# Filter sums in the first transform stage, tap and cross sums by accumulating transfers, a fused gate, and a second norm turned by transfers

## The chip, the cores and the metric

One Trainium2 chip, one core. The metric is device time of one execution in microseconds (us). TensorE is called PE here, VectorE DVE, ScalarE ACT, GpSimd POOL, SyncE SP, as the profile calls them. POOL and SP also issue transfers: POOL's are the profile's queue q0 (software), SP's the queue q1 (hardware).

## The reference, cut to what matters

A layer norm, a convolution block with a gate, a residual, a second layer norm and a SwiGLU feed-forward block, on a sequence of S = 2048 rows of D = 640 columns.

```python
x = A_q                                          # [1, 2048, 640]
k_shift[s] = sum over t of k[s - 3 + t] * shift_k[:, 3 - t]      # four taps
kv = k_shift * v
y  = causal convolution of kv with ssm_k along S, + kv * ssm_D    # by FFT in the reference
h  = x + layernorm(x) * y
out = h + (silu(layernorm(h) @ w_gate) * (layernorm(h) @ w_up)) @ w_down    # F = 1728
```

## The kernel before, in words

The sequence is cut into four blocks of 512 rows (j = 0 to 3), the columns of the convolution into two halves of 320 (c = 0, 1). A tile holds 512 rows as 128 partitions x 4 rows. The causal convolution works on spectra of 1024 points: block j of the output needs the products of the spectra X(i) of kv and K(m) of the filter with i + m = j, and K(m) must stand for filter blocks m and m-1 together.

For each block and half the kernel goes through these steps.

- **Taps** (`kv_block`, line 909): four products of 1280 columns and three sums, all on DVE through the helper at line 756, and one product with v. One block-half is eight DVE instructions.
- **Filter** (`load_kraw`, line 614): the filter block is turned by a transposing transfer (line 620) and laid out again by way of DRAM (`k_nat`).
- **First transform stage** (`fwd`, line 670): 8 matmuls of 320 columns per tile, evacuations on ACT, then four shuffles within SBUF by transfers on SP's queue. **Second stage** (`spec`, line 741): 4 matmuls for each of four groups of frequencies (h = 0 to 3).
- **Filter sum** (`shift_add`, line 747): two DVE instructions of 640 columns add the spectra of filter blocks j and j-1.
- **Products** (`products`, line 758; `combine`, line 792): complex products of 1280 columns, added up on DVE over the pairs (i, m). Block 2 also computes two pairs ahead for block 3. Then `inv2` and `conv_bp` transform back.
- **Gate and residual** (`conv_bp`, line 1006): ACT (or DVE) makes layernorm(x) (line 877), DVE multiplies it with y from PSUM (640 columns) and adds the residual (640 columns).
- **Second norm** (`ln_bp`, line 1051): the normalised rows are turned by 10 PE transposes (line 1063) and copied out of PSUM by ACT or DVE into HNT.
- **Feed-forward** (`ffn_pair`, `ffn_b`, lines 1090 and 1126): for a block, 135 matmuls of 512 columns and 112 of 320, with SiLU on ACT (line 1103) and a product of 1024 columns on DVE.

Block 0 has a dense transform instead (`dense_c`, line 708). Its tables lie in the space of spectra that are not used yet. PSUM is cut into two pools of two slots, pF for the feed-forward and pC for the convolution.

The order of all instructions is written out at build time by a list planner in the kernel (`Prog.schedule`, line 131). It gives each operation a cost, a priority (1000 j + 100 c + ... for the convolution, 10000 + 100 j for the feed-forward) and, for transfers, a modelled landing. Each engine and each queue then runs its list strictly in order, waiting at an instruction until what it depends on is done. On POOL that list holds the loads of k, v, x and of all weights, each weight piece waiting for the piece two before it, and the power instruction of the layer norms (line 867). So whatever waits on POOL holds all loads behind it.

```python
def piece(subs, kb, cells, nm):
    chain.append(dma(subs, kb, [], cells, 35, eng="pool", after=chain[-2:-1] or [kv_last[0, 0]], name=nm))
```

Of the kernel before, what the change touches and what calls it, by code (L numbers as in the profile page):

```python
# [40 lines left out]
class Prog:  # L41
# [196 lines left out]
    def emit(self, nc, es, block, ndma_sems):  # L238
# [4 lines left out]
        for e in self.ENG:  # L243
            n = 0
# [23 lines left out]
        for e in self.ENG:  # L268
            prog, seen, owed = [], {}, 0
            for o in self.order[e]:  # L270
# [15 lines left out]
                for tl in {x[0] for x in o.writes}:  # L286
                    for p in tl.prev:
                        wrote = any(x[0] is not None and x[0].base == tl.base and x[0].pool == tl.pool for x in p.writes)
                        need(p, 2 if wrote else 1)
# [54 lines left out]
def _tables(R):  # L344
# [4 lines left out]
    for T in range(2):  # L349
        f1 = (64 * T + np.arange(64))[None, :] + 0.5  # L350
        s1f[:, T, 0:64] = np.cos(2 * np.pi * q * f1 / 256)
        s1f[:, T, 64:128] = -np.sin(2 * np.pi * q * f1 / 256)
    s1i = np.stack([s1f[:, T, :].T for T in range(2)], axis=1)
# [18 lines left out]
    cols = [s1f.reshape(128, -1), s1i.reshape(128, -1), w2s, w2i.reshape(128, -1), np.eye(128)]  # L372
# [31 lines left out]
def bass_sequential_preLN__ssm_conv_h3__swiglu_ffn__prompt_kernel(  # L404
# [18 lines left out]
    tab_np, (oS1, oS1I, oW2, oW2I, oID) = _tables(R)  # L423
# [8 lines left out]
    with ExitStack() as es:  # L432
        NEL = 102720
        sb = es.enter_context(nc.sbuf_tensor("sb", [128, NEL], bf))
        tab = es.enter_context(nc.sbuf_tensor("tab", [128, tab_np.shape[1]], f16))
        stt = es.enter_context(nc.sbuf_tensor("stt", [128, 192 + 32 + 192 + 8], f32))
        ps = es.enter_context(nc.psum_tensor("ps", [128, 4096], f32))
        psb = ps[:].bitcast(bf)
        cur = [0]
# [10 lines left out]
        def V(t, off, n, p0=0, p1=128):  # L450
            return sb[p0:p1, t.base + off:t.base + off + n]

# [44 lines left out]
        P.pool("TMP", slots(2, 4 * CW), True)  # L497
        P.pool("KRAW", slots(1, 3 * B), True)
        P.pool("KT", slots(2, 4 * CW), True)
        P.pool("TK", slots(2, 8 * CW), True)  # L500
        P.pool("TX", slots(3, 8 * CW), True)
        sx, sxb = slots(2, 8 * CW), slots(2, 8 * CW)
        skb, sk = slots(2, 8 * CW), slots(2, 8 * CW)
        P.pool("SX", sx + sxb, True)
        P.pool("SK", sk + skb, True)
        DEN = P.tile("den", None, sxb[0])
# [7 lines left out]
        P.pool("SS", slots(5, 4 * CW), True)  # L514
        P.pool("PP", slots(3, 4 * CW), True)
        P.pool("P0", [HNT.base + i * 2 * CW for i in range(4)], True)
        P.pool("EP", slots(3, 2 * CW), True)
        P.pool("JK", slots(1, 2 * CW), True)
        P.pool("pF", [0, 1024])
        P.pool("pC", [2048, 3072])  # L520
# [55 lines left out]
        for k in range(4):  # L576
            def tap(k):
                pt = P.tile("ptap", "pC" if k % 2 else "pF")
# [35 lines left out]
        def load_kraw(j, c, prio):  # L614
# [11 lines left out]
            if (j, c) == (0, 1):  # L626
                t = kraws[j, c] = P.tile("kraw01", None, GUT.base + 11 * CW)
            else:
                t = kraws[j, c] = P.tile(f"kraw{j}{c}", "KRAW")
# [10 lines left out]
        def k_natural(j, c, prio):  # L640
# [6 lines left out]
            pt = P.tile("pKT", "pC")  # L647
# [22 lines left out]
        def fwd(nm, srcs, pool, prio):  # L670

            tbt = P.tile("TB" + nm, pool)
            for b in range(4):
                pt = P.tile("p1", "pC")
# [23 lines left out]
        def dense_h(nm, src, h, dst, prio):  # L698
            pt = P.tile("pd", "pC")
# [8 lines left out]
        def dense_c(c):  # L708
# [7 lines left out]
            acc = [P.tile(f"y{c}{i}", "pF") for i in range(2)]  # L716
            for h in range(R):
                dense_h(f"X{c}", vins[0, c], h, xt, pb + 103)
                a1, a2 = products([(xt, h * 640, kt, h * 640)], [h], "P0", pb + 110, f"0{c}{h}")
                combine((a1, a2), lambda a1=a1: V2(a1, 0, 640, 1, CW), lambda a2=a2: V2(a2, 0, 640, 1, CW), 1, [(a1, 0)], [(a2, 0)],  # L720
                        pb + 110, f"0{c}{h}")
                fns = []
                for ri, a in enumerate((a1, a2)):
                    for b in range(R):
                        fns.append(mm(lambda b=b: B32(acc[b // 2], b % 2, CW), lambda h=h, ri=ri, b=b: den(oIV(h, ri, b)),
                                      lambda a=a: V(a, 0, CW), h == 0 and ri == 0, h == R - 1 and ri == 1))
                last = pe(fns, CW, 8, [(a1, 0), (a2, 0), (DEN, ("i", h))], [(acc[0], 0), (acc[1], 0)], pb + 110, name=f"di{c}h{h}")
# [13 lines left out]
        def spec(nm, r, u, h, dst, off, prio):  # L741
            pt = P.tile("p2", "pC")
            pe(stage2(u, h, pt), CW, 2, [(u, h), (TAB, 1)], [(pt, 0)], prio, reserve=[(dst, h)], name=f"s2{r}{nm}h{h}", mode=1)
            evac(lambda: V2(dst, off, CW, 2, CW), lambda: B32x2(pt, CW), 2 * CW, [(pt, 0)], [(dst, h)], prio,
                 name=f"e2{r}{nm}h{h}", after=[den_last[0]])

        def shift_add(dst, do, cur_, co, prv, po, hs, prio, nm):
            rd = [(t, h) for t in (cur_, prv) for h in hs]
            wr = [(dst, h) for h in hs]
            o1 = vec(dve2(640), tt(lambda: V2(dst, do, 960, 2, CW), lambda: V2(cur_, co, 960, 2, CW), lambda: V2(prv, po + CW, CW, 2, CW), ALU.subtract),  # L750
                     rd, [(dst, (h, "a")) for h in hs], prio, name=f"ks{nm}")
            vec(dve2(640), tt(lambda: V2(dst, do + CW, CW, 2, CW), lambda: V2(cur_, co + CW, CW, 2, CW), lambda: V2(prv, po, 960, 2, CW), ALU.add),
                rd + [(dst, (h, "a")) for h in hs], wr, prio, name=f"kp{nm}")
# [4 lines left out]
        def products(terms, hs, pool, prio, nm):  # L758


            n = len(hs)
            accs = None
            for n_, (xt, xo, kt, ko) in enumerate(terms):
                p1 = P.tile(f"P1{nm}", pool)
                p2 = P.tile(f"P2{nm}", pool) if n_ == 0 else None
                rd = [(xt, h) for h in hs] + [(kt, h) for h in hs]

                def m1(dst, xt=xt, xo=xo, kt=kt, ko=ko, rd=rd):
                    vec(dve2(640 * n), tt(lambda: V(dst, 0, 640 * n), lambda: V(xt, xo, 640 * n), lambda: V(kt, ko, 640 * n), ALU.mult),
                        rd, [(dst, i) for i in range(n)], prio, name=f"m1{nm}")  # L770

                def m2(dst, xt=xt, xo=xo, kt=kt, ko=ko, rd=rd):
                    vec(dve2(640 * n), tt(lambda: V3(dst, 0, 640, n, CW, 2, CW), lambda: V3(xt, xo, 640, n, CW, 2, CW),
                                          lambda: V3(kt, ko + CW, 640, n, -CW, 2, CW), ALU.mult),
                        rd, [(dst, i) for i in range(n)], prio, name=f"m2{nm}")

                def add(a, b_):
                    vec(dve2(640 * n), tt(lambda: V(a, 0, 640 * n), lambda: V(a, 0, 640 * n), lambda: V(b_, 0, 640 * n), ALU.add),
                        [(t, i) for t in (a, b_) for i in range(n)], [(a, i) for i in range(n)], prio, name=f"ac{nm}")

                m1(p1)
                if n_ == 0:
                    m2(p2)
                    accs = (p1, p2)
                else:
                    add(accs[0], p1)
                    q2 = P.tile(f"P2{nm}", pool)
                    m2(q2)
                    add(accs[1], q2)
            return accs  # L790

        def combine(accs, dre, dim, n, wre, wim, prio, nm, after=()):
            a, b_ = accs
            ra, rb = [(a, i) for i in range(n)], [(b_, i) for i in range(n)]
            o1 = vec(dve2(CW * n), tt(dre, lambda: V2(a, 0, 640, n, CW), lambda: V2(a, CW, 640, n, CW), ALU.subtract),
                     ra, wre, prio, name=f"cr{nm}")
            vec(dve2(CW * n), tt(dim, lambda: V2(b_, 0, 640, n, CW), lambda: V2(b_, CW, 640, n, CW), ALU.add),
                rb, wim, prio, name=f"ci{nm}", after=[o1])
# [440 lines left out]
```

## Time and profile before

| what | value |
|---|---|
| times of three runs | 325.8, 326.7 (median), 331.81 us |
| span of the profiled execution, first to last instruction | 329.1 us |
| busy: PE, DVE, ACT, POOL | 284.9, 251.0, 184.7, 40.8 us |
| 1280-column DVE instructions on SBUF | 176, 140.3 us busy |
| 640-column DVE instructions on SBUF | 96, 44.7 us busy |
| first instruction of the feed-forward of block 0 / 1 / 2 / 3 | 64.9 / 137.9 / 225.2 / 281 us |
| end of the last matmul | 325.9 us |

The profiled execution's own total is not listed beside its span; its span is 2.4 us above the median of the times. The columns of the table of windows are: stretch, its length, busy time and (x instructions) of PE, PEld (weight load), DVE, ACT and POOL, the granted PE clock as a share of full speed, the busy share of the transfer engines, and GB/s. In a timeline a line is: start, length, engine, line, operation, output<-input, count, and in brackets the idle time before it and what ended that. "128x1280" is partitions x elements. Since two instructions of an engine overlap a little, the distance from start to start (the pitch) is smaller than the duration of one.

### The profile page before, as it was taken

How to read it: one execution, taken by the hardware profiler on the slowest of the kernel's cores; microseconds unless marked ns; L12 is line 12 of the kernel's file. 1: busy time of each engine (PE TensorE's matmuls, PEld its weight loads, DVE VectorE, ACT ScalarE, POOL GpSimd, SP SyncE). 2: the span in 40 equal slices, each digit the busy share in tenths (PEclk: the TensorE clock that was granted, in tenths of full speed). 3: DMA queues.
4: the chain of work that ended last, by engine and by line, in shares of the span. 5: the costliest groups of instructions: out<-in, count | busy, mean ns of one | idle time of the engine just before them, and what ended most of it. 6: DMA issues, size and time to landing. Idle time of an engine off the chain costs nothing.

```text
span 329.1 us, 4717 instructions
## 1 busy us (share of the span) xinstructions
PE 284.9 (87%) x1724; PEld 151.7 (46%) x1740; DVE 251.0 (76%) x441; ACT 184.7 (56%) x293; POOL 40.8 (12%) x55
## 2 busy tenths in 40 slices
PE   3999773787999999999989971648999999999996
PEld 1567441443444366644436640223444477444474
DVE  1969997579799999699999799998499955222322
ACT  4388986875658854875748462578755214112200
POOL 2513235321100202100010000021000001000000
PEclk9999795589899999999999995556999999999999
DMA  7998859989794533331111213321110111000011
GB/s 197 348 393 262 249 170 331 126 258 240 211 271 118 179 132 120 118 114 41 65 57 38 96 67 120 120 82 40 51 72 0 43 60 42 20 0 2 0 42 40
DMA packets 33099, 40.57 MB, mean 123 GB/s; under 512 B 10472, under 2 KB 28291, under 8 KB 33076
## 3 DMA queue, kind: packets, MB, share of 16 engines
q1 hardware_dynamic: 28932, 25.57, 25.4%
q0 software_dynamic: 3296, 14.01, 14.7%
q10 hardware_dynamic: 848, 0.69, 0.8%
q8 instruction: 14, 0.23, 0.3%
q14 instruction: 9, 0.07, 0.1%
HBM read 21.91 MB, written 4.59 MB: 81 GB/s over the span
## 4 chain that ended last, share of the span: by engine, by line
PE 40%; DVE 36%; DMA 15%; issue 4%; ACT 3%; POOL 2%; ACTq 0%; SPq 0%; POOLq 0%; DVEq 0%
PE ps L559 39%; DVE sb L756 33%; DMA sb<-sb 6%; DMA sb<-in_A_k_dram 6%; ACT sb L542 2%; DMA sb<-in_A_ssm_k_dram 2%; DMA sb<-in_B_w_gate_dram 2%; DVE stt L851 1%; POOL sb L550 1%; PE ps L656 1%; ACT sb L545 1%; DVE sb L1023 0%; POOL stt L867 0%; PE ps L1063 0%; POOL sb L666 0%
## 5 line engine op out<-in xcount | busy, mean ns | idle before, releaser
L559 PE MATMUL ps<-sb 128*128 128x320 bf16 (+2 forms) x1188 | 224.2, 343 | 9.4 <-DMA sb<-in_A_shift_k_dram 2.4
L756 DVE TENSOR_TENSOR sb<-sb 128x1280 bf16<-128x1280 bf16 (+1 forms) x288 | 181.2, 683 | 28.7 <-DMA sb<-in_A_k_dram 12.3
L559 PEld LDWEIGHTS ps<-sb 128*128 128x128 bf16 (+2 forms) x1204 | 116.6, 100 | 103.4 <-issue 10.9
L542 ACT ACTIVATE sb<-ps 128x640 bf16<-128x640 f32 (+1 forms) x131 | 90.4, 729 | 47.4 <-PE ps L559 41.6
L559 PE MATMUL ps<-sb,tab 128*64 128x320 bf16 (+2 forms) x432 | 62.0, 341 | 25.3 <-DMA sb<-sb 8.6
L756 DVE TENSOR_TENSOR sb<-ps,sb 128x1024 bf16<-128x1024 f32 (+3 forms) x52 | 50.2, 982 | 42.2 <-PE ps L559 40.0
L559 PEld LDWEIGHTS ps<-sb,tab 128*64 128x64 f16 (+2 forms) x432 | 26.7, 110 | 59.2 <-issue 22.1
L1103 ACT ACTIVATE sb<-ps 128x1024 bf16<-128x1024 f32 (+2 forms) x32 | 29.3, 916 | 43.6 <-PE ps L559 43.3
L877 ACT ACTIVATE sb<-sb,stt 128x320 bf16<-128x320 bf16 (+1 forms) x40 | 27.3, 728 | 14.4 <-DVE stt L869 11.9
L867 POOL TENSOR_TENSOR stt<-stt 128x2 f32<-128x2 f32 (+1 forms) x12 | 12.6, 1054 | 111.7 <-DVE stt L905 60.3
L545 ACT ACTIVATE sb<-ps 128x640 bf16<-128x640 f32 x24 | 15.6, 701 | 6.0 <-PE ps L559 6.0
L889 ACT ACTIVATE sb<-sb 128x640 bf16<-128x640 bf16 x16 | 11.9, 742 | 6.3 <-DMA sb<-in_A_q_dram 6.2
L896 ACT ACTIVATE sb<-sb,stt 128x640 bf16<-128x640 bf16 x16 | 13.2, 826 | 3.6 <-DVE stt L892 3.4
L851 DVE BATCH_NORM_STATS2 stt<-sb 128x6 f32<-128x320 bf16 x32 | 13.5, 477 | 0.0
L1063 PE MATMUL ps<-sb 128*128 128x128 bf16 x80 | 7.8, 265 | 3.7 <-DVE stt L869 3.1
L550 POOL DMA_DIRECT2D sb<-in_A_k_dram x6 | 5.9, 990 | 35.6 <-DVE sb L756 35.6
L550 POOL DMA_DIRECT2D sb<-in_A_v_dram x6 | 4.7, 775 | 45.5 <-PE ps L559 42.6
L1063 PEld LDWEIGHTS ps<-sb 128*128 128x128 bf16 x80 | 6.5, 120 | 6.0 <-ACT sb L877 3.6
L656 PE MATMUL ps<-sb 128*128 128x128 bf16 (+1 forms) x24 | 4.1, 282 | 2.6 <-DMA sb<-in_A_ssm_k_dram 2.6
L550 POOL DMA_DIRECT2D sb<-in_B_w_down_dram x6 | 4.3, 724 | 15.3 <-DMA sb<-in_B_w_down_dram 11.9
L656 PEld LDWEIGHTS ps<-sb 128*128 128x128 bf16 (+1 forms) x24 | 2.0, 118 | 5.2 <-DMA sb<-in_A_ssm_k_dram 3.2
L543 DVE COPY sb<-ps 128x1280 bf16<-128x1280 bf16 x3 | 2.5, 818 | 2.4 <-PE ps L1063 2.4
(24 smaller groups left out, 37.5 us busy)
## 6 DMA issues: line engine op xcount, KB each, us to landing
sb<-sb SPq DMA_DIRECT2D x72, 160.0 KB, 2.2
sb<-in_A_k_dram POOLq DMA_DIRECT2D x6, 560.0 KB, 6.3
out_dram<-sb SPq DMA_DIRECT2D x16, 160.0 KB, 1.8
sb<-in_B_w_gate_dram POOLq DMA_DIRECT2D x5, 416.0 KB, 5.5
sb<-in_B_w_up_dram POOLq DMA_DIRECT2D x5, 416.0 KB, 6.5
sb<-cst_den SPq DMA_DIRECT2D x8, 256.0 KB, 7.1
sb<-in_A_q_dram POOLq DMA_DIRECT2D x3, 640.0 KB, 5.6
sb<-in_A_v_dram POOLq DMA_DIRECT2D x6, 320.0 KB, 4.1
```

Source lines behind the costliest of these rows:

```text
L542: fns = {"act": lambda a: a.activation(out=dst(), in_=src(), func=ACTF.Copy), "dve": lambda v: v.tensor_copy(out=dst(), in_=src())}
L545: fns = {"act": lambda a: a.activation(out=dst(), in_=src(), func=ACTF.Copy, scale=scale), "dve": lambda v: v.tensor_scalar(out=dst(), in0 ...
L550: fns = [(lambda g, d=d, s=s: g.dma_start(d(), s())) for d, s in subs]
L559: return lambda t: t.matmul(o(), l(), r(), start=st, stop=sp)
L756: return lambda v: v.tensor_tensor(out=o(), in0=a(), in1=b_(), op=op)
L851: vec(dve1(CW, False), lambda v: v.bn_stats(st6(l, j, b, c), V(xt, b * D + c * CW, CW)), [(xt, (b, c))], [(ST, ("s", l, j, b, c))], prio, ...
L867: P.op({"pool": 1.05}, lambda g: g.tensor_tensor(out=y, in0=va, in1=stt[:, 420:420 + hi - lo], op=ALU.pow), c1 + [(ST, "half")], c3, prio, ...
L877: "act": lambda a: a.activation(out=dst(), in_=src(), func=ACTF.Identity, scale=rs(l, j, b), bias=tmv(l, j, 3)[:, b:b + 1])},
L889: P.op({"act": act_c(D) + 0.22}, lambda a, b=b, jt=jt: a.activation(out=V(jt, 0, D), in_=V(xt, b * D, D), func=ACTF.Copy, accum_out=tmv(l, ...
L896: P.op({"act": act_c(D) + 0.3}, lambda a, b=b, jt=jt: a.activation(out=V(jt, 0, D), in_=V(xt, b * D, D), func=ACTF.Square, bias=tmv(l, j, ...
L1063: fns.append(lambda t, k=k, d=d: t.transpose(B16(pt, k, d * 128, 128), V(hn[k], d * 128, 128), V(IDN, 0, 128)))
L1103: P.op({"act": act_c(n)}, lambda a: a.activation(out=dst(), in_=src(), func=ACTF.Silu), rd, wr, -1000, name=f"si{j}{i}")
```

## The change

- **Filter sum**: the first stage for K now takes two sources, filter blocks j and j-1, the second with a table of its own (`s1p`), accumulating in PSUM: 16 matmuls for a tile where there were 8. `shift_add` is gone.
- **Tap sums** for j = 1 to 3: three accumulating transfers of 320 KB on POOL's queue (`dma_add`) in place of three DVE sums. The third waits for the first two, and the fourth tap product needs a slot that the first accumulation frees. Block 0 keeps its DVE sums.
- **Cross sums** of block 2: (0,2) + (1,1) and, for block 3, (1,2) + (2,1), as accumulating transfers of 640 KB, two for each half and pair of h, eight in all. One DVE sum of 2560 columns joins the part computed ahead to the block's own product.
- **Gate**: ACT writes w = y * (SCALE * rstd) + 1 in f32 from PSUM (320 columns, 8 per block), DVE does h' = (x - mean) * w in one instruction of 320 columns. The mean left out is given back at the end of `ffn_b`.
- **Second norm** for j = 1 to 3: each of the four 128 x 640 tiles is turned by a transposing transfer on SP's queue into HNT. Block 0 keeps the PE transposes.
- **Storage**: one PSUM pool of four slots; the dense tables lie where w_down comes later, so w_down waits for the last dense matmul.

```diff
+        def dma_add(a, b_, w, ca, cb, prio, nm):
+            P.op({"pool": 1.0}, [lambda g: g.dma_start(V(a, 0, w), V(b_, 0, w), max_dma_last_dim=2560, accum_op=ALU.add)],
+                 [(a, k) for k in ca] + [(b_, k) for k in cb], [(a, k) for k in ca], prio, dma=(w * 0.256, "acc"), name=f"da{nm}")
...
         def kv_block(j, c, prio):
...
+            def add(a, b_):
+                if j:
+                    dma_add(a, b_, W4, [0], [0], prio, f"k{j}{c}")
+                    return
+                vec(dve2(W4), tt(lambda: V(a, 0, W4), lambda: V(a, 0, W4), lambda: V(b_, 0, W4), ALU.add), ...)
...
+            t0, t1 = mul(0), mul(1)
+            add(t0, t1)
+            t2 = mul(2)
+            if j:
+                t3 = mul(3)
+                add(t2, t3)
+                add(t0, t2)
...
-            shift_add(kt, ko, st, so, pv, po, hs, pr, f"{nm}{h0}")
...
-            uk = fwd(f"K{j}{c}", [(kts[j, c], oS1)], "TK", pb + 104)
+            uk = fwd(f"K{j}{c}", [(kts[j, c], oS1), (kts[j - 1, c], oS1P)], "TK", pb + 104)
...
+            ahead = prod(0, j, pr - 3, "a")
+            if j == 2:
+                more = prod(1, 1, pr - 3, "b")
+                dma_add(ahead, more, 1280 * n, both, both, pr - 3, f"a{j}{c}{h0}")
+            own = prod(j, 0, pr, "o")
+            add_into(own, ahead, n, pr, f"{j}{c}{h0}")
+            combine_own(own, n, pr, f"{j}{c}{h0}")
...
             if j == 2:
+                a3 = prod(1, 2, pr + 3, "c")
+                b3 = prod(2, 1, pr + 3, "d")
+                dma_add(a3, b3, 1280 * n, both, both, pr + 3, f"c{c}{h0}")
...
+                P.op({"act": act_c(CW, True)}, lambda a, k=k, b=b, wt=wt: a.activation(
+                    out=VF(wt, CW), in_=B32(pt, k, CW), func=ACTF.Identity, scale=tmv(0, j, 3)[:, b:b + 1], bias=stt[:, oCO:oCO + 1]), ...)
+                vec(dve1(CW), lambda v, b=b, wt=wt, xv=xv: v.scalar_tensor_tensor(
+                    out=xv(), in0=xv(), scalar=tmv(0, j, 5)[:, b:b + 1], in1=VF(wt, CW), op0=ALU.add, op1=ALU.mult), ...)
...
+                if j:
+                    P.op({"sp": 1.3}, [lambda g, t=t, b=b: g.dma_start_transpose(out=V2(HNT, b * 128, 512, 5, 128), in_=V(t, 0, D))],
+                         [(t, 0)], [(HNT, (d, b)) for d in range(5)], pr, dma=(164, "turnh"), name=f"tr{j}{b}")
```

The planner writes a new order. POOL's list around the middle, in the changed kernel (k21 is the k tile of block 2, half 1; "taps 11 a/b/c" are the three accumulations of block 1, half 1):

```
load k10, w_gate0, w_up0, x1, v10, w_gate1, taps 10 a, w_up1, power, w_gate2, load k11, taps 10 b, w_up2, w_gate3,
taps 10 c, w_up3, w_gate4, power x2, w_up4, w_up rest, load v11, taps 11 a, power, w_gate rest, w_down, w_down,
taps 11 b, w_down, load k20, w_down, taps 11 c, w_down, w_down rest, taps 20 a, load v20, load k21, taps 20 b,
taps 20 c, load v21, cross, taps 21 a, load k30, taps 21 b, power x2, taps 21 c, cross, taps 30 a, cross, ...
```

On PE the feed-forward of block 1 now lies between the second stages of block 2, that of block 2 starts after the back transform of block 3's first half, and after the feed-forward of block 2 only that of block 3 follows, with nothing between.

More of the change, by code (lines that the diff above doesn't have):

```diff
@@ L287, in emit @@
                     for p in tl.prev:
-                        wrote = any(x[0] is not None and x[0].base == tl.base and x[0].pool == tl.pool for x in p.writes)
-                        need(p, 2 if wrote else 1)
+                        need(p, 2)
                 if o in extra:
@@ L352, in _tables @@
         s1f[:, T, 64:128] = -np.sin(2 * np.pi * q * f1 / 256)
+    s1p = np.zeros((128, 2, 128))
+    for T in range(2):
+        f1 = (64 * T + np.arange(64))[None, :] + 0.5
+        s1p[:, T, 0:64] = np.cos(2 * np.pi * (q - 128) * f1 / 256)
+        s1p[:, T, 64:128] = -np.sin(2 * np.pi * (q - 128) * f1 / 256)
     s1i = np.stack([s1f[:, T, :].T for T in range(2)], axis=1)
@@ L755, in tt, with products @@
         def tt(o, a, b_, op):
             return lambda v: v.tensor_tensor(out=o(), in0=a(), in1=b_(), op=op)
-        def products(terms, hs, pool, prio, nm):
+        def products(xt, xo, kt, ko, hs, pool, prio, nm):
             n = len(hs)
[L762 to L798, printed above, removed]
+            p = P.tile(f"P{nm}", pool)
@@ L1052, in ln_bp @@
             xt = xts[j]
-            pt = P.tile("p5", "pC")
             hn = []
```

235 lines of the change are left out of this document (117 added, 118 removed).

## The prediction

> **What bounds the kernel now.** I read the page first (busy shares, slices, chain), then the table of windows cut where the slices change, then the timelines of DVE and POOL, then the transfers.
>
> ```profile
> PE 284.9 (87%) x1724; PEld 151.7 (46%) x1740; DVE 251.0 (76%) x441; ACT 184.7 (56%) x293; POOL 40.8 (12%) x55
> ...
> PE   3999773787999999999989971648999999999996
> ...
> DVE  1969997579799999699999799998499955222322
> ...
> PEclk9999795589899999999999995556999999999999
> DMA  7998859989794533331111213321110111000011
> ...
> PE 40%; DVE 36%; DMA 15%; issue 4%; ACT 3%; POOL 2%; ACTq 0%; SPq 0%; POOLq 0%; DVEq 0%
> ```
>
> DVE is full from the start to slice 27, PE from slice 9 to the end, with two holes: slices 5 to 10 and 23 to 27, where the granted clock drops too.
>
> ```profile
> 46.00:73.00 27.00, 17.64 (x101) 8.15 (x100) 19.78 (x46) 21.35 (x36) 9.88 (x13) 0.68 0.96 228
> 73.00:127.00 54.00, 50.32 (x305) 24.47 (x307) 50.83 (x77) 34.16 (x51) 4.76 (x6) 0.97 0.70 194
> ...
> 188.00:225.00 37.00, 20.04 (x129) 10.00 (x129) 34.03 (x67) 22.23 (x39) 3.56 (x4) 0.63 0.25 89
> ...
> 245.00:329.00 84.00, 80.04 (x486) 44.81 (x489) 38.44 (x62) 20.69 (x25) 1.41 (x2) 1.00 0.07 24
> ```
>
> From 46 to 73 the transfers are full (0.96): weights and tiles arrive. From 73 on DVE and PE are both over 90% busy. From 188 to 225 PE waits for DVE (34.0 of 37.0 busy). After 245 only PE counts. So DVE work taken out before 225 is worth time, down to the point where PE has no hole left.
>
> ```profile
> 96.95 1.55 DVE L756 TENSOR_TENSOR sb<-sb 128x1280 bf16<-128x1280 bf16 x2
> ```
>
> Pitches come from such lines: two 1280-column instructions take 1.55 us, one alone 0.82, so each costs 0.74. In the same way 640 columns cost 0.40, 1024 from PSUM 1.14, 640 from PSUM 0.73, 320 of statistics 0.40. On PE 112 matmuls of 320 columns in 15.39 us make 0.136 each, 512 columns 0.214, the halved ones of the second stage 0.081.
>
> ```profile
> 55.61 0.97 POOL L550 DMA_DIRECT2D sb<-in_A_k_dram  x1
> 57.55 0.79 POOL L550 DMA_DIRECT2D sb<-in_B_w_down_dram  x1 [0.98 <-DMA sb<-in_B_w_up_dram]
> ...
> 59.36 0.80 POOL L550 DMA_DIRECT2D sb<-in_B_w_down_dram  x1
> 69.31 0.76 POOL L550 DMA_DIRECT2D sb<-in_B_w_down_dram  x1 [9.15 <-DMA sb<-in_B_w_down_dram]
> ```
>
> POOL's queue stands still while a weight piece lands: 9.15 us here. The k tile issued at 55.61 got out before that.
>
> ```profile
> sb<-sb SPq DMA_DIRECT2D x48, 160.0 KB, 2.1
> ...
> sb<-in_A_q_dram POOLq DMA_DIRECT2D x2, 640.0 KB, 4.8
> ...
> sb<-in_A_v_dram POOLq DMA_DIRECT2D x3, 320.0 KB, 3.5
> ...
> sb<-in_A_ssm_k_dram SPq DMA_TRANSPOSE x1, 3.5
> ```
>
> These are issue to landing after 100 us, when the transfers are quiet; over the whole run the transposing transfer has 5.9 in the median.
>
> **What is removed from DVE.** 18 tap sums (13.3 us) and 16 cross sums of block 2 (11.8) at 0.74; 24 filter sums at 0.40 (9.6); three copies out of PSUM at 0.75, against one evacuation that now falls to DVE (1.5). The gate had 16 x 0.73 + 16 x 0.40 and 4 normalisations at 0.28 (19.2), and gets 32 instructions of 320 columns in f32. None such is in the trace: 0.40 (statistics on 320 columns) to 0.73 (640 columns from PSUM) each; I take 0.42, near the first, as the column count is equal: 5.8 gained (4.2 lost at the upper end). The f32 writing on ACT replaces 28 normalisations of 0.65; from PSUM 640 columns take 0.70, so it is below that, and ACT has room (34 of 54 us). All in all DVE falls from 244 to about 201 us of pitch.
>
> **What is added.** PE: 48 first-stage matmuls at 0.136 (6.5) less 60 transposes at 0.056 (3.4). POOL: 26 accumulations, each an issue of 0.55 to 0.8 as the loads show. SP: 12 transposing issues at 1.4, 5.6 in a row for a block with shuffles and stores queued behind; SP stood waiting for most of the span, so I cost its issue at nothing.
>
> **Price of an accumulation.** None is in the trace. Lower end: the 160 KB copies within SBUF, 2.1. Upper end: twice the POOL loads (two operands are read), 7.0 for 320 KB and 9.6 for 640 KB. The POOL loads of the same size lie nearest, 3.5 and 4.8; I add a tenth for the second read, 3.8 and 5.3. The Trainium skill ("DMA: Bandwidth & Descriptors", Anatomy of one DMA) gives a fit of 2.0 us + bytes / 436 GB/s for transfers issued from POOL, an estimate of 2.75 and 3.5 here; the loads in the trace took 3.5 and 4.8, so the trace is above it, and by the fit the sum below would be 302 instead of 313.
>
> **The sum, in three stages of the new order.**
>
> Stage 1, to the arrival of block 2's first k tile (k20), which DVE needs to go on. In the new list the first accumulation waits for DVE's second tap product, at about 30 us, and holds w_up1 (at 25.2 before) to 31. The fourth product waits for that accumulation, under load 5.8 like the v tile: DVE idles some 3 us, and the third accumulation holds w_up3 to 46 (42.5 before). DVE has 6 us less to do up to block 0's second norm, so that comes 4 to 5 us earlier and the feed-forward of block 0 starts near 62 (64.9). But the first w_down goes out at 59 (57.55), the third waits 10.9 for it, and k20 stands behind that third one: issued at 70.7, landing after 6.3 (the median of k tiles), at 77. Before it was issued at 55.6 and landed at 67.7. Ends: 68, if the queue moves as before, and 83, if k20 takes its 12.05 again. The tap sums of block 1's second half are in the same queue and come at 78; PE waits with DVE.
>
> Stage 2, from there DVE's list up to the last input of block 3's back transform: 81 of 1280 columns (59.9), 9 of 2560 (1.42 each by the slope of 0.53 ns per column, 12.8), 26 of 640 (10.4), 11 of 1024 and 4 of 512 from PSUM (14.9), 16 gate instructions (6.7), 16 statistics (6.4), 24 small (2.1): 113. Before, the same stretch held 150. PE's work beside it is 112, so PE is hidden by DVE and its waits, with nothing to spare.
>
> Waits of DVE in stage 2. For each accumulation I add up what stands on DVE between its last operand and its user. The eight cross sums have 12, 5.9, 3.0, 4.8, 4.2, 1.6, 3.8 and 2.6 us; at 5.3 that leaves waits of 11.8. Tap sums: the fourth product comes 1.9, 1.9, 4.5 and 4.2 after the second, at 3.8 two waits of 1.9; two in a row before the last product (7.6) find 9.6, 11.9, 7.4 and 17.7, a wait of 0.2. Together 15.8. With the ends: 1 and 70. To this the late k31 tile (1.2) and the waits for PE and ACT that DVE has now in this stretch (1.0 + 1.5 + 0.6 + 1.8 + 0.6 + 0.5 = 6): 23.
>
> Stage 3, PE alone: from that back transform 270 matmuls of 512 columns, 272 of 320 and 48 halves, 98.8 us, then 0.8 for the last sum and 2.4 for its store as before. Second norm of block 2: four transposing transfers after it, each between half of 3.5 and 3.5, so 7 to 14 in a row, while DVE and PE need 9.9 + 7.4 = 17.3 before the feed-forward asks for them. Covered; block 1 has 20, block 3 the whole feed-forward of block 2.
>
> 77 + 113.3 + 23 + 98.8 + 3.2 = 315.3 as a span, against 329.1. The profiled span stands 2.4 above the median of the times, so **313 us**.
>
> **Rivals.**
> - *The accumulations are quick.* They land like the 320 KB and 640 KB loads or sooner and k20 comes at 70 to 74: waits of 8 to 19, 291 to 306. For it: quiet transfers after 127 us (share 0.23 and less). Against: stage 1 is not quiet.
> - *The gain is eaten on the queues.* k20 at 83 and 28 of waits: 324, no change that can be measured (a measurement of this kernel can tell about 2%, 320.2 to 333.2). Or the transposing transfers keep the 5.9 of the median each: 23.6 + 1 for four, 7 beyond the cover in block 2 and up to 5 in block 1, 320 to 325. The Trainium skill ("VectorE: DVE Perf Modes", The three transpose paths) speaks for this: 1309 ns for 128 x 128 by the transfer crossbar against 390 on TensorE, 26 us by estimate for the 20 squares of a block, 10 beyond the cover. The trace's 10 squares in 3.5 us are a quarter of that, so I give this part only 0.05.
> - *The other side: the accumulations are slow.* Every microsecond in them is a wait of an in-order DVE. From 4.8 us for 320 KB and 7.4 for 640 KB on (waits of 35) the kernel is slower by 2%; at 5.5 and 8.0 it is 342, at twice the loads 367. For it: two operands are read, stage 2 has no other slack. Against: the loads of the same queue beside a DVE 94% busy (73 to 127 us) are well below.
>
> **How the numbers follow.** Forecast 0.42 with 307 to 320 of its own; quick accumulations 0.18; gain eaten 0.20; slow accumulations 0.20. Faster by over 2%: 0.60, within: 0.20, slower: 0.20. The range 299 to 338 leaves out the lower part of the quick case and the upper part of the slow one, some 0.2.
>
> **What would show it.** Accumulations of 3.5 to 4 and 5 to 5.5 us in the transfer list; DVE waits "<-DMA sb<-sb" of about 16 us where there are none now; DVE's wait for in_A_k near 70 to 77; DVE pitch near 201; PE's hole at 188 to 225 gone and the feed-forward of block 2 starting near 221. Wrong would be a wait of PE for the transposing transfers, a feed-forward of block 0 that starts after 66, or accumulations above 7 us.

## The result, and the profile after

The changed kernel takes 354.25 us in the median (350.46 to 362.27, four runs) against 327.63 us for the kernel before: a ratio of 1.080, interval 1.072 to 1.089. It is slower, where 313 us were forecast. The profiled execution took 354.32 us with a span of 352.4. Some executions run slower, mostly at a lower granted clock: of the runs 1, 5 and 13 below only the lowest time is free of that and stands beside the median, the free executions of run 6 and of the changed kernel have medians of 322.77 and 354.18 us, and of the profiles of 1, 2, 5, 7, 12, 13 and 18 only single rows are used.

The page of the changed kernel, the lines that answer to those of before:

```profile
PE 289.6 (82%) x1711; PEld 153.0 (43%) x1728; DVE 211.0 (60%) x363; ACT 183.5 (52%) x293; POOL 65.6 (19%) x82
...
PE   4999624397969989949749699799878899999996
...
DVE  2978754377438949856558479695293862222422
...
PEclk9999985869899999998969679999999999999999
DMA  8999998999697585998992751744312004100001
...
q0 software_dynamic: 8064, 25.15, 30.9%
...
PE 36%; DMA 34%; DVE 15%; SPq 5%; issue 5%; ACT 4%; POOL 0%; DVEq 0%; POOLq 0%; ACTq 0%
```

DVE lost the work it was to lose: 211.0 us busy for 251.0. But it is now never full for long, and neither is PE. The DMA row stays mostly at 7 to 9 up to slice 21, where it fell to 5 and less from slice 13 on before, and the chain that ended last has 34% of DMA in it for 15%. The software queue (q0: packets, MB, share) was busy for 14.7% of 329.1 us, 48 us; now it is 30.9% of 352.4, 109 us, for 11.1 MB more. Before, that queue and the shuffles stood so:

```profile
q0 software_dynamic: 3296, 14.01, 14.7%
...
sb<-sb SPq DMA_DIRECT2D x72, 160.0 KB, 2.2
```

The table of windows, cut as in the prediction (stretch, length, busy time of PE, PEld, DVE, ACT, POOL, granted clock, transfer share, GB/s; the share is worked out from packet times and can come out above 1):

```profile
46.00:73.00 27.00, 11.01 (x68) 5.87 (x68) 12.19 (x30) 15.28 (x24) 10.99 (x14) 0.69 1.11 213
73.00:127.00 54.00, 46.30 (x255) 20.95 (x259) 38.66 (x52) 33.48 (x50) 12.08 (x14) 0.90 0.83 219
127.00:188.00 61.00, 46.69 (x283) 25.21 (x285) 41.44 (x68) 30.59 (x50) 16.84 (x18) 0.92 0.87 200
188.00:225.00 37.00, 31.75 (x164) 13.44 (x163) 26.57 (x42) 22.86 (x36) 6.12 (x6) 0.86 0.51 124
...
252.00:353.00 101.00, 92.71 (x521) 49.36 (x526) 43.30 (x68) 32.68 (x51) 3.05 (x4) 1.00 0.11 35
```

The line of 127 to 188 before:

```profile
127.00:188.00 61.00, 59.57 (x382) 32.23 (x385) 56.08 (x96) 39.68 (x64) 5.94 (x6) 1.00 0.22 73
```

From 127 to 188 the same 61 us held 59.57 us of PE and 56.08 of DVE before, at a transfer share of 0.22. Now PE has 46.69 and DVE 41.44: both are idle for part of the time, and the transfers are nearly full (0.87) at only 200 GB/s. PE loses 13 us here, 4 from 73 to 127 and 7 from 46 to 73; the old hole at 188 to 225 has shrunk (31.75 for 20.04). From 252 on only PE counts, as before.

The transfers by kind (issue by, count, KB each, median us from issue to landing), and who waited for them (us in total, times, longest):

```profile
sb<-sb SPq DMA_DIRECT2D x72, 160.0 KB, 3.7
sb<-sb POOLq DMA_DIRECT2D x18, 320.0 KB, 6.2
sb<-sb POOLq DMA_DIRECT2D x8, 640.0 KB, 6.2
...
sb<-in_A_q_dram POOLq DMA_DIRECT2D x3, 640.0 KB, 8.9
...
sb<-sb SPq DMA_TRANSPOSE x12, 2.4
```

```profile
DVE sb L751 <- DMA sb<-sb: 37.7, 16, 6.1
```

```profile
POOL sb L770 <- DMA sb<-sb: 33.2, 6, 9.0
```

The accumulations took 6.2 us in the median, of either size. That mixes stretches: three of the eight large ones lie between 188 and 225 us, where the transfers are half empty (0.51) and they took 5.6. From 127 to 188 us alone:

```profile
sb<-sb SPq DMA_DIRECT2D x16, 160.0 KB, 3.6
sb<-sb POOLq DMA_DIRECT2D x8, 320.0 KB, 6.1
sb<-sb POOLq DMA_DIRECT2D x4, 640.0 KB, 7.3
```

Not only the accumulations are slow: over the run the shuffles, which SP issues, went from 2.2 to 3.7, the x tiles from 5.6 to 8.9. The transposing transfers of the second norm are quick.

Two starts on PE, the first feed-forward of block 0 and of block 2 (64.90 and 225.22 before):

```profile
76.05 6.76 PE L563 MATMUL ps<-sb 128*128 128x512 bf16 x29 [0.22 <-ACT sb L546]
...
252.44 4.26 PE L563 MATMUL ps<-sb 128*128 128x512 bf16 x19 [0.35 <-ACT sb L546]
```

### The profile page after: what moved, and what is told of

Read it like the earlier page. It is cut to its first block, busy times and chain, and to the rows that moved or that the text cites. A ratio compares the mean times of both kernels' runs of the same rounds, so it can differ in the third digit from the quotient of the medians.

```text
span 352.4 us, 4706 instructions
## 1 busy us (share of the span) xinstructions
PE 289.6 (82%) x1711; PEld 153.0 (43%) x1728; DVE 211.0 (60%) x363; ACT 183.5 (52%) x293; POOL 65.6 (19%) x82
## 3 DMA queue, kind: packets, MB, share of 16 engines
q0 software_dynamic: 8064, 25.15, 30.9%
## 4 chain that ended last, share of the span: by engine, by line
PE 36%; DMA 34%; DVE 15%; SPq 5%; issue 5%; ACT 4%; POOL 0%; DVEq 0%; POOLq 0%; ACTq 0%
PE ps L563 36%; DMA sb<-sb 18%; DVE sb L751 12%; DMA sb<-in_A_ssm_k_dram 10%; SPq L554 4%; DMA k_nat<-sb 3%; DMA sb<-in_A_q_dram 3%; ACT sb L546 2%; DVE sb L1011 1%; DVE stt L836 1%; SPq L624 1%; ACT sb L1089 1%; ACT sb L887 1%; ACT sb L1007 0%; ACT sb L880 0%
## 5 line engine op out<-in xcount | busy, mean ns | idle before, releaser
L751 DVE TENSOR_TENSOR sb<-sb 128x1280 bf16<-128x1280 bf16 (+3 forms) x198 | 136.6, 743 | 66.5 <-DMA sb<-sb 37.7
L546 ACT ACTIVATE sb<-ps 128x640 bf16<-128x640 f32 x143 | 95.1, 725 | 47.5 <-PE ps L563 36.0
L563 PE MATMUL ps<-sb,tab 128*128 128x320 bf16 (+2 forms) x480 | 68.6, 332 | 41.5 <-DMA sb<-sb 12.8
L563 PEld LDWEIGHTS ps<-sb,tab 128*128 128x128 f16 (+2 forms) x480 | 31.0, 108 | 78.2 <-issue 27.2
L751 DVE TENSOR_TENSOR sb<-ps,sb 128x1024 bf16<-128x1024 f32 (+2 forms) x32 | 34.5, 1085 | 38.2 <-PE ps L563 31.3
L770 POOL DMA_DIRECT2D sb<-sb x26 | 26.0, 1009 | 83.4 <-DVE sb L751 42.5
L1007 ACT ACTIVATE sb<-ps,stt 128x320 f32<-128x320 f32 x32 | 17.8, 619 | 9.9 <-DVE sb L1011 8.2
L1137 DVE SCALAR_TENSOR_TENSOR sb<-ps,stt,sb 128x640 bf16<-128x640 f32 x8 | 7.1, 883 | 23.0 <-PE ps L563 23.0
L852 POOL TENSOR_TENSOR stt<-stt 128x2 f32<-128x2 f32 (+1 forms) x12 | 12.3, 1033 | 42.6 <-DVE stt L851 31.5
L1011 DVE SCALAR_TENSOR_TENSOR sb<-sb,stt 128x320 bf16<-128x320 bf16 x32 | 16.2, 541 | 5.0 <-ACT sb L1007 5.0
L868 ACT ACTIVATE sb<-sb,stt 128x640 bf16<-128x640 bf16 x12 | 10.8, 916 | 10.4 <-DVE stt L860 7.7
L887 ACT ACTIVATE sb<-sb,stt 128x640 bf16<-128x640 bf16 x16 | 13.2, 827 | 2.3 <-DVE stt L883 2.1
L554 POOL DMA_DIRECT2D sb<-in_A_k_dram x6 | 6.1, 1014 | 10.7 <-DVE sb L1011 8.7
```

Of the source, the lines that this page charges most:

```text
L546: fns = {"act": lambda a: a.activation(out=dst(), in_=src(), func=ACTF.Copy), "dve": lambda v: v.tensor_copy(out=dst(), in_=src())}
L554: fns = [(lambda g, d=d, s=s: g.dma_start(d(), s())) for d, s in subs]
L563: return lambda t: t.matmul(o(), l(), r(), start=st, stop=sp)
L751: return lambda v: v.tensor_tensor(out=o(), in0=a(), in1=b_(), op=op)
L770: P.op({"pool": 1.0}, [lambda g: g.dma_start(V(a, 0, w), V(b_, 0, w), max_dma_last_dim=2560, accum_op=ALU.add)], [(a, k) for k in ca] + [( ...
L852: P.op({"pool": 1.05}, lambda g: g.tensor_tensor(out=y, in0=va, in1=stt[:, oCO + 4:oCO + 4 + hi - lo], op=ALU.pow), c1 + [(ST, "half")], c ...
```

## The experiments

Theory A: the accumulations cost the transfer engines far more than their bytes, hold DVE and POOL in their order, and slow every other transfer. Rival B: the rest of the change (K's longer path, storage, one PSUM pool, transposing transfers) is the cause. The planner writes a new order for every kernel in which an operation is added, removed or priced otherwise; runs 5, 6 and 13 leave its order exactly as it is in the changed kernel, and are the cleanest.

### 1 to 4: parts taken back

Runs 1 to 3 replace `dma_add` by the DVE sums, for the taps, the cross sums, and both; run 4 also turns the second norm on PE again.

```diff
-                if j:
-                    dma_add(a, b_, W4, [0], [0], prio, f"k{j}{c}")
-                    return
...
-                dma_add(ahead, more, 1280 * n, both, both, pr - 3, f"a{j}{c}{h0}")
+                add_into(ahead, more, n, pr - 3, f"a{j}{c}{h0}")
```

> The changed kernel with the tap sums of blocks 1 to 3 back on DVE (18 of 0.74 us, 13.3 us more of pitch); the cross sums stay accumulating transfers. Theory A (accumulations load the transfer engines and hold DVE and POOL in order; both kinds share the blame by bytes, 5.9 MB of taps against 5.2 MB of cross sums, and the taps also hold the weights on POOL, which put the first feed-forward 11 us later): 328 to 338 us, first feed-forward back to about 65. Rival B (the accumulations are not the cause, but the rest: K path by two sources, the new storage, the transposing transfers): 345 to 358, first feed-forward still after 72.

> The changed kernel with the cross sums of block 2 on DVE (8 sums of 2560 columns at 1.42 us, 11.4 us more of pitch); the tap sums stay accumulating transfers. Theory A: the full transfers between 120 and 190 us ease, shuffles fall below 3 us there, 338 to 346 us; the first feed-forward stays at 76, since nothing changes before it. Rival B: 350 to 362.

> The changed kernel with no accumulating transfer at all: tap and cross sums on DVE. What stays is the filter sum in the first stage, the fused gate, the transposing transfers of the second norm and the storage. DVE's pitch is 226 us against 244 before and 201 in the changed kernel. Theory A: 312 to 322 us, faster than before, as DVE has 18 us less and the transfers are as empty as before (shuffles near 2.2 us). Rival B: 338 to 352, no better than the changed kernel by more than 5 per cent.

> As the run without accumulations, and the second norm of blocks 1 to 3 turned on PE again (60 transposes, 3.4 us of PE, and six evacuations on ACT or DVE). Theory A, with the transposing transfers harmless (2.4 us each in the changed kernel): 2 to 6 us slower than the run without accumulations. Rival C (the transposing transfers hold the shuffles and the feed-forward): 3 to 10 us faster than it.

Measured: run 1 357.63 us (lowest 348.24), run 2 350.98 (ratio 1.079, 1.071 to 1.087), run 3 332.95 (1.030, 1.022 to 1.038), run 4 342.92 (1.058, 1.050 to 1.065). Taking back one half of the accumulations gains next to nothing, taking back both gains 21 of the 27 us (by the ratios, 5 of the 8%). So theory A has most of it, but its numbers for runs 1 and 2 were missed: the loss does not add up by bytes, shuffles stay at 3.4 us in run 2, and the feed-forward of block 0 starts at 70.38 in run 1 and 83.41 in run 2, not at 65 and 76. Why half of the sums cost nearly as much as all of them is not shown. Run 3 stays 3% above the kernel before, though its DVE is 18 us less busy (232.7 for 251.0). So rival B has a part too. Rival C fell: without the transposing transfers the kernel is 10 us slower, not faster, which is also more than theory A's 2 to 6.

### 5 and 6: the same order, cheaper transfers

```diff
-            ... g.dma_start(V(a, 0, w), V(b_, 0, w), max_dma_last_dim=2560, accum_op=ALU.add)
+  run 5:    ... g.dma_start(V(a, 0, w), V(b_, 0, w), max_dma_last_dim=2560)
+  run 6:    ... g.dma_start(V(a, 0, w // 4), V(b_, 0, w // 4), max_dma_last_dim=2560, accum_op=ALU.add)
```

> The changed kernel, with its order of instructions unaltered; the 26 accumulating transfers copy instead of adding (the sums are left out, so the output is another). Theory A (an accumulation costs the transfer engines about twice a copy of the same bytes: while one ran alone they moved 205 to 215 GB/s, the x load 360 to 430): software queue's share falls from 30.9 to about 23 per cent, 640 KB land in under 4.5 us where transfers are quiet (5.5 with adding), time 335 to 345 us. Rival D (any transfer from SBUF to SBUF of this size costs that, the adding is free): share, landings and time as in the changed kernel, 349 to 356.

> The changed kernel, order unaltered; each accumulation takes a quarter of its columns (80 and 160 KB; three quarters of the sums are left out, so the output is another). Issue, queue and waits are the same, the bytes are a quarter. Theory A (bytes on the transfer engines and the landing times that follow are the cause): landings near 3 us, DVE waits for accumulations under 15 us in sum, time 318 to 332. Rival E (the fixed price: the issue on POOL, the queue that stands behind each, the planned order): 342 to 352.

Measured: run 5 339.70 us (lowest 329.69); run 6 324.61, ratio 0.988 (0.980 to 0.996). In run 5 the copies landed in 5.0 and 3.9 us for 6.2 and 6.2:

```profile
q0 software_dynamic: 5888, 25.15, 24.6%
...
sb<-sb SPq DMA_DIRECT2D x72, 160.0 KB, 3.5
sb<-sb POOLq DMA_DIRECT2D x18, 320.0 KB, 5.0
sb<-sb POOLq DMA_DIRECT2D x8, 640.0 KB, 3.9
```

24.6% of 339.0 is 83 us. Less the 48 of the loads, the 11.1 MB took 35 us of the transfer engines as copies and 61 as sums (if the loads took 48 in both): adding costs some 1.7 times a copy. It is seen most plainly where a transfer runs alone. First the changed kernel from 200 to 220 (40 slices of 0.5 us; the sum issued at 205.79 is in the first run of nines after slice 15), then run 5 from 190 to 215 (0.625 us each; a copy issued at 195.09 is in slices 11 to 13):

```profile
DMA  9930093810000009999994000100000000000268
GB/s 382 359 113 0 0 152 108 360 36 0 0 0 0 0 0 189 215 205 205 220 195 82 0 0 0 33 0 0 0 0 0 0 0 0 0 0 0 92 238 323
...
sb<-sb POOLq DMA_DIRECT2D x2, 640.0 KB, 5.5
```

```profile
DMA  9200087000896000000000000289998406777770
GB/s 363 90 0 0 7 194 299 25 0 0 377 410 262 0 0 26 0 0 0 0 0 0 0 0 0 82 320 424 412 369 313 178 12 254 258 262 262 262 262 13
...
sb<-sb POOLq DMA_DIRECT2D x2, 640.0 KB, 3.6
```

Alone, a copy moves 377 to 410 GB/s and a sum 189 to 220, with the engines 80 to 90% busy or more in both: 5.5 us for 640 KB against 3.6. Rival D fell.

Run 6 has a quarter of the bytes:

```profile
q0 software_dynamic: 7040, 16.80, 21.4%
...
sb<-sb SPq DMA_DIRECT2D x72, 160.0 KB, 2.5
...
sb<-sb POOLq DMA_DIRECT2D x18, 80.0 KB, 3.9
sb<-sb POOLq DMA_DIRECT2D x8, 160.0 KB, 3.1
```

```profile
DVE sb L751 <- DMA sb<-sb: 12.1, 7, 6.9
```

Some 30 us are gone with three quarters of the bytes, in the same order of instructions, with the same issues and waits. Part of the difference is in PE's clock: the 1711 matmuls in each trace keep PE busy for 278.7 us here, at a mean granted clock of 0.979, and for 289.6 in the changed kernel, at 0.932. No run holds the clock fixed, so whether it fell because PE waited is not shown. Rival E (fixed price, queue, order) keeps what is left, and that is not little: with DVE as empty as in the changed kernel (209.7 us) and small sums, the kernel is only 1.2% faster than before. Part of that is in the chain of run 6, in the stage where the transfers are full (0.9 to 1.0 up to 80 us):

```profile
30.70 4.69 DMA sb<-sb
...
37.76 11.37 DMA sb<-sb
```

A tap sum of 80 KB took 11.4 us there. Its own bytes can't be the reason (the median of that size is 3.9); from 37 to 50 us a w_up and a w_gate piece on the same queue took 12.3 and 11.7 us as well.

### 7: the planner told the true price

```diff
             if kind == "acc":
-                return issued + 3.0
+                return issued + 6.5
```

> The changed kernel, only the planner's model of an accumulation altered: it lands 6.5 us after its issue instead of 3.0, so the planner puts other work between. Theory A (load on the transfer engines is the larger part): 338 to 350, DVE's waits for accumulations shorter, shuffles still above 3 us. Rival F (only the wrong price in the plan): 315 to 332.

Measured: 367.66 us, 1.126 (1.115 to 1.137). Rival F fell, and theory A's number too: it is 13 us worse than the changed kernel. DVE's waits for sums did fall (25.9 us for 37.7), the order found around them was worse in other places. A new order alone cost 13 us here, so single differences of that size between re-planned kernels (runs 1 to 4, 8 to 12 and 14 to 18) are to be read with care.

### 13: the load without the wait

Run 6, and behind each quarter sum, on the same queue, a DRAM-to-DRAM copy of the bytes taken away, for which nobody waits before the end of the kernel:

```diff
+                g.dma_start(dram(x_dram.ap(), i * 128 * 1920, [[n, 128], [1, n]]), dram(B_w_up, 0, [[n, 128], [1, n]])).then_inc(spare_sem, 16)
```

> The run with quarter accumulations (324.6 us, three quarters of the sums left out), order unaltered, and behind each accumulation on the same queue a copy from DRAM to DRAM of the three quarters of the bytes that were taken away, for which nobody waits. Theory L (the load slows the shuffles, loads and turned tiles, and that costs the 30 us): 340 to 355, shuffles near 3.7 us again. Theory W (the waits of DVE for the accumulations cost it): 325 to 335, shuffles slow but DVE's waits for accumulations near 12 us as in the quarter run.

Measured: 351.22 us (lowest 343.26). Against 322.77 us for run 6 and 354.18 for the changed kernel the 343.26 brings 20 of 31 us back; against their lowest times (319.51 and 350.46) 24 of 31. It is a single execution.

```profile
q0 software_dynamic: 7872, 25.15, 28.2%
...
sb<-sb SPq DMA_DIRECT2D x72, 160.0 KB, 4.4
...
sb<-sb POOLq DMA_DIRECT2D x18, 80.0 KB, 4.7
sb<-sb POOLq DMA_DIRECT2D x8, 160.0 KB, 2.9
```

```profile
DVE sb L753 <- DMA sb<-sb: 19.5, 9, 9.8
```

The sums themselves are small again and DVE waits 19.5 us for them, not 37.7, though more than the 12.1 of run 6; the shuffles are at 4.4. PE's waits for transfers within SBUF in runs 6 and 13 and in the changed kernel:

```profile
PE ps L563 <- DMA sb<-sb: 6.0, 6, 2.5
```

```profile
PE ps L565 <- DMA sb<-sb: 14.9, 11, 3.2
```

```profile
PE ps L563 <- DMA sb<-sb: 12.8, 8, 5.3
```

Theory L has the larger part: two thirds to three quarters of the loss return with a load that DVE does not wait for, some of it still as DVE's wait for the small sums. The four kernels with the same order make a row (queue q0's time less 48 us for the loads, an estimate; times as above, those of 5 and 13 single executions):

| run | time of the engines for sums and their stand-ins | DVE's waits for sums | time |
|---|---|---|---|
| 6 | 20 us | 12.1 us | 322.8 us |
| 5 | 35 us | 23.3 us | 329.7 us |
| 13 | 51 us | 19.5 us | 343.3 us |
| changed kernel | 61 us | 37.7 us | 354.2 us |

The time follows the engines' time, not DVE's waits. It does not follow the median of the shuffles either (2.5, 3.5, 4.4 and 3.7), so which of the slowed transfers costs most is not shown. What run 13 can't part is POOL: 26 more issues make it 77.1 us busy for 63.0.

### 8 to 11 and 15: parts added to the kernel before

Turning transfers alone (8), filter sum in the first stage alone (9), fused gate alone (10), all three (11), the first two (15); storage, PSUM pools and DVE sums as before. The edits are those of the change, put into the old kernel.

> The kernel before, with one part of the change alone: the second norm of blocks 1 to 3 is turned by transposing transfers instead of PE transposes. If they are worth in the kernel before what they were without accumulations (10 us), 312 to 320 us. Rival G (their worth there came from ACT and from the one PSUM pool, which the kernel before does not have): 322 to 328, no difference of 2 per cent.

> The kernel before with the filter sum in the first transform stage alone (24 DVE sums of 640 columns gone, 9.6 us; 48 matmuls more, 6.5 us). Theory H (the middle of the kernel before is bound by DVE, so DVE's 9.6 us count, less what PE loses): 316 to 322 us. Rival I (PE has no room beside DVE there, it was over 90 per cent busy from 73 to 188, and K's first stage gets longer; the gain is eaten): 325 to 333.

> The kernel before with the fused gate and residual alone (5.8 us of DVE pitch gone, ACT writes 32 tiles of 320 columns in f32 in place of 28 normalisations). Theory H: 319 to 325 us. Rival I (the gate lies on a chain through PE, ACT and DVE at the end of each block and now has ACT in it before every DVE instruction): 326 to 332.

> The kernel before with three parts of the change: filter sum in the first stage, fused gate, second norm by transposing transfers; storage, PSUM pools and sums by DVE as before. DVE's pitch falls by some 19 us. Theory H: 308 to 318 us, faster than both kernels. Rival I (as the changed kernel without accumulations, 333, which has the same parts in the new storage and order): 326 to 335.

> The kernel before with the filter sum in the first stage and the turning transfers, gate as before. Alone they gave 0.992 and 0.996, the gate alone 1.012, the three together 0.994. If parts add up: 320 to 323 us (0.982 to 0.990). If the order the planner finds matters more than the parts: 324 to 330.

Measured: run 8 0.996 (0.990 to 1.001), run 9 0.992 (0.986 to 0.997), run 10 1.012 (1.007 to 1.018), run 11 0.994 (0.990 to 0.998), run 15 0.987 (0.979 to 0.995). The parts add up within their intervals. Theory H's gains did not come: runs 9 and 11 (323.91 and 324.54 us) lie between H and I, run 10 (328.36) in rival I's range, run 8 (325.01) in rival G's. The gate costs. Its page (the same line of before has DVE 251.0 and ACT 184.7):

```profile
PE 284.7 (87%) x1740; PEld 149.7 (46%) x1740; DVE 249.8 (77%) x440; ACT 187.9 (58%) x296; POOL 41.6 (13%) x56
```

The 5.8 us of DVE that it was to free are 1.2 in the page: a gate instruction took 0.54 us, where 0.42 of pitch were costed. ACT has 3 us more.

### 12, 14 and 16: PSUM in two pools

```diff
-        P.pool("PS", [0, 1024, 2048, 3072])
+        P.pool("pF", [0, 1024])
+        P.pool("pC", [2048, 3072])
```

Run 12 has no accumulations, run 14 has them, run 16 is run 12 with the gate as before.

> The changed kernel without accumulating transfers (333 us) and with PSUM in two pools of two slots as in the kernel before, instead of one of four. Theory J (the single pool lets the feed-forward and the convolution hold each other's slots and costs the gain): 318 to 327. Rival K (the pool does not matter): 329 to 338.

> The changed kernel with its accumulations, PSUM in two pools of two slots as in the kernel before. If the single pool costs there what it cost without accumulations (11 us): 338 to 346. If the accumulations hide it (DVE and the transfers set the pace): 348 to 358.

> The changed kernel without accumulations, with two PSUM pools (0.984 of the kernel before) and with the gate as before. If the fused gate costs here what it cost alone (1.2 per cent): 314 to 319 us. If it gains here (DVE 5.8 us less): 323 to 330.

Measured: run 12 321.99 us, 0.984 (0.976 to 0.993), against 332.95 with one pool; run 14 349.17, 1.069 (1.060 to 1.077); run 16 316.36, **0.9705 (0.963 to 0.978)**, faster than both kernels. Theory J's range came true where the accumulations are gone; where they are there, most of the gain is hidden. The fused gate cost 1.4% again (run 12 to run 16). One place where the single pool may show is a wait of DVE for ACT in run 3 (one pool); the changed kernel has it too, with 10.41 us, and run 6 with 10.4:

```profile
230.74 4.56 DVE L751 TENSOR_TENSOR sb<-sb 128x1280 bf16<-128x1280 bf16 x5 [10.92 <-ACT sb L546]
```

In run 12 DVE's longest wait for that line is 1.5 us, and the first feed-forward starts at 61.77 (63.32 in run 16) instead of 68.72. The order is another one too, so what of the 11 us is the slots and what the order that came with them is not parted. Run 16 has PE at 90% of its span:

```profile
PE 284.2 (90%) x1728; PEld 150.7 (48%) x1728; DVE 237.7 (76%) x394; ACT 180.0 (57%) x286; POOL 40.4 (13%) x56
```

### 17 and 18: a few sums where transfers are quiet

Run 16 with only block 3's tap sums (17), or only the four cross sums made ahead for block 3 (18), as accumulating transfers.

> Base 316.4 us; only the tap sums of block 3 (6 of 320 KB, 1.9 MB) become accumulating transfers, 4.4 us less of DVE's pitch, where the base's transfers are one fifth to three fifths busy. Theory A (it was the load that cost, and here it is small): 312 to 317. Rival M (the price of one, 5 us and more in a chain of three between DVE's instructions, costs whatever the load): 318 to 326.

> Base 316.4 us; only the four cross sums that block 2 makes ahead for block 3 (640 KB each, 2.6 MB) become accumulating transfers, 5.7 us less of DVE's pitch; nobody needs them before block 3. Theory A: 311 to 317. Rival M (they wait on POOL before the loads of x and v, and hold product slots): 318 to 326.

Measured: run 17 318.45 us, 0.980 (0.972 to 0.988), at the lower edge of rival M's range and within the noise of run 16; run 18 328.11, 1.009 (1.005 to 1.012), above both expectations. Run 17 gains nothing, though its sums land as forecast for quiet transfers:

```profile
sb<-sb POOLq DMA_DIRECT2D x6, 320.0 KB, 3.8
```

Run 18's four sums took 6.3 us in the median. But its order had lost time before the first of them was issued, at 136.24: from 80 to 100 us PE is busy for 14.1 us, in run 16 for 20.0. So it settles nothing about the sums themselves.

## Why the prediction was wrong, point by point

- **DVE's pitch, 244 to 201: right.** Busy time fell by 40.0 us where 42 to 43 of pitch were summed (the terms give 42, the two totals 43). The gate instruction was a little dearer (two of them take 1.01 us, one 0.53), the filter and tap terms held.
- **Price of an accumulation, 3.8 and 5.3: the step that failed first.** Quiet, it is right: 3.8 in run 17, 5.5 in the quiet stretch of the changed kernel. But the price was taken from loads of the kernel before after 100 us (share 0.22 from 127 to 188), and used in a stretch that the accumulations themselves fill (0.87). There it was 6.1 and 7.3, and 7.9 for the tap sums issued before 73 us. The tenth added for the second read should have been a doubling of the engines' time: 189 to 220 GB/s for 377 to 410.
- **What the sum has no term for: the load on the others.** The prediction priced an accumulation as a wait of DVE alone. Run 13 shows that 20 to 24 of 31 us are lost with most of that wait gone, at shuffles of 4.4 us. This is the larger part of the miss. The check was at hand: in the kernel before 14.01 MB of loads took 48 us of the transfer engines, so 11.1 MB more are 38 us by estimate even at the rate of a load; they took 61.
- **Stage 1, one wait of 3 us, feed-forward of block 0 near 62: wrong.** DVE waited 13.9 us for sums before 76 us, and the feed-forward started at 76.05, after the 66 that was named as a sign. POOL stood 8.96 us before the third tap sum, with w_up3 and the rest of the weights behind it. The sums are not the whole reason: run 3 has none and starts at 68.72, run 14 has them and two PSUM pools and starts at 63.53. The wait, and the issue of k20:

```profile
48.34 0.89 POOL L770 DMA_DIRECT2D sb<-sb  x1 [8.96 <-DMA sb<-sb]
...
74.66 1.03 POOL L554 DMA_DIRECT2D sb<-in_A_k_dram  x1
```

  The k tile k20 was issued at 74.66 (70.7 forecast), but DVE did not wait for it; its waits for k tiles are 6.0 us in all, from the start of the kernel.
- **Stage 2, waits of 15.8 us for sums, 6 for PE and ACT: too small.** From 76 to 242 us DVE waited 23.8 us for sums, 10.2 for PE and 10.7 for ACT, and then 10.4 more for ACT (the wait named under run 12). So the waits for PE and ACT were missed by more (15 us) than those for the sums (8 us).
- **"PE's work beside it is hidden", DVE's microseconds at face value: the step that failed second.** Run 6, with small sums, has DVE 41 us emptier than before and gains 1.2%; runs 9 to 11 have 1 to 12 us less of it busy (243.6, 249.8 and 239.5 for 251.0) and change the time by -0.8, +1.2 and -0.6%. In run 9 PE is busy for 114 of the 115 us from 73 to 188 (110 before), so there was no room beside it for DVE's gain. In the changed kernel itself neither engine is full there; how much of its miss is owed to this step is not shown.
- **Stage 3, PE alone: nearly right.** The feed-forward of block 2 was to start near 221, 94 us before the end of the span at 315.3. It started at 252.44, 100.0 us before the end, and PE was busy for 92.71 of the last 101 us. So 31 of the 37 us by which the span was missed lie before it.
- **From span to time, minus 2.4: doubtful.** In every run on record the time stands 1.6 to 2.2 us above its span. The profiled execution of the kernel before thus took some 331 us, 4 above the median, and the step may be some 4 us too low. That is small beside the miss of 41.
- **Transposing transfers, 1.75 to 3.5 each, covered: right.** 2.4 in the median, and PE starts the feed-forward of block 2 on an evacuation, not on them. The 1309 ns that the Trainium skill ("VectorE: DVE Perf Modes", The three transpose paths) gives for one 128 x 128 square would by estimate make 6.5 us of the five squares of one transfer; the trace, at 2.4, disagrees. Their worth is open: 10 us by run 4, none to be measured in run 8.
- **The rival that came true** is the slow accumulation. It had the wait of DVE and not the load: put into the prediction's own gaps, 6.1 and 7.3 us make waits of 45 us and a time of 342 (an estimate). Measured were waits of 23.8 and a time of 354.
- **The single PSUM pool had no term, and the fused gate was costed as a gain of 5.8 us of DVE.** Runs 3 and 12 differ by 11 us for the pool and its order; the gate cost 1.4% between runs 12 and 16 and 1.2% in run 10. SP's issues, costed at nothing, are 5% of the chain (SPq) of the changed kernel and 0% before.

The Trainium skill ("DMA: Bandwidth & Descriptors", Issuing engines are not separate DMA queues) says that transfers of all issuing engines run on the same 16 and interleave. The runs agree: in the same order of instructions SP's shuffles took 2.5 us in run 6, 3.7 in the changed kernel with more bytes issued by POOL, and 4.4 in run 13.

## What to carry to other kernels

Before work is moved to the transfer engines, sum up their time in the stage where it lands as one does for a compute engine, at the rate of that kind of transfer, and price everything else that is under way there at the loaded time. An engine's saved microseconds count only until the next engine beside it is full, so check what busy share the forecast asks of that one. And where a planner writes the order, test causes with kernels that keep it.

## What the runs showed of the hardware that was not expected

- An accumulating transfer within SBUF keeps the transfer engines over 90% busy at half the rate of a copy: 189 to 220 against 377 to 410 GB/s alone, some 61 against 35 us of engine time for 11.1 MB.
- Its time depends less on its size than on what else is under way: in the changed kernel 640 KB took 7.3 us from 127 to 188 us and 5.5 from 200 to 220, 320 KB took 7.9 before 73 us and 6.1 from 127 to 188; in run 6 one of 80 KB took 11.4 us, at a median of 3.9.
- Five 128 x 128 squares are turned by one transposing transfer in 2.4 us from issue to landing (3.5 in run 16, medians).
- The 1711 matmuls in each trace kept PE busy for 278.7 us at a mean granted clock of 0.979 (run 6) and for 289.6 us at 0.932 (changed kernel).
